# Block-sorted attention and a squared-ReLU layer: output transposes by DMA, later loads, earlier sorting

## The chip, the cores and the metric

One core of a Trainium2 chip runs the whole program. The metric is device time in microseconds of one execution; 14 executions of the kernel before gave a median of 249.14 us (247.87 to 253.91). The engines are TensorE (PE; its weight loads are shown as PEld), VectorE (DVE), ScalarE (ACT), GpSimd (POOL) and SyncE (SP). SP and POOL issue DMAs. Each engine takes its instructions in program order.

## The reference

Four batches, eight heads, 768 tokens, head dimension 64, eight blocks of 96 tokens. `sort_net` is normalised over rows and columns five times, and the resulting 8x8 matrix P of each head mixes the blocks of keys and values. Each query block attends to its own mixed block. The heads' outputs are joined to 3072 rows of 512, and a layer 512 -> 2048 -> 512 with a squared ReLU follows:

```
for _ in range(5):
    P = exp(P - max(P, -1)); P = P / (sum(P, -1) + 1e-9); P = P / (sum(P, -2) + 1e-9)
k_sorted = einsum('bhij,bhjcd->bhicd', P, k_b);  v_sorted = einsum('bhij,bhjcd->bhicd', P, v_b)
attn = softmax(q_b @ k_sorted.T / sqrt(64))      # per block
x = (attn @ v_sorted) as [3072, 512]
out = (s * relu(x @ w_in)**2 + b) @ w_out
```

## The kernel before

The 3072 rows are eight half batches t = 0 to 7 of 384 tokens (four blocks of 96); batch b has t = 2b and 2b+1. Matrix products take bf16 operands.

**Keys and values.** `load_k`, `load_v` and `load_q` (lines 78 to 92) read float32 from DRAM on POOL's queue and write bf16. `k_piece` (L278 and its casts) multiplies raw keys by a block-diagonal matrix built from P: `pd1` for batches 0 and 1, `pd2` for 2 and 3, and leaves sorted, transposed keys in `ks`. With nb = 2 one piece serves batches 2 and 3 together (128 columns); with nb = 1 it serves one batch (64 columns). Pieces with more than 8 groups of 64 columns take their PSUM tile from `psa` (three buffers of two banks), smaller ones from `psb` (two buffers of one bank). `v_piece1` (L320, batch 1) and `v_piece2` (L334, batches 2 and 3) sort values; the result goes through DRAM (`dv`) and `v_read` (L345) brings it back to `VS[b]` with the tokens on the partitions.

**Attention of a half batch t.** `q_piece` (L259) transposes q on TensorE into `QT`; `s_piece` (L359) makes scores, ACT the exponential (L362); `p_piece` (L386) multiplies by the sorted values, DVE divides by the sum (L390, L391) into `X[t]`, 96 partitions x four blocks x 512. `t_piece` (L414) transposes `X[t]` on TensorE, sixteen 96x128 blocks into one psa tile, and `evac` (L228 on DVE, L230 on ACT) copies it to `XT[t]` with the 512 features on the partitions.

**Dense layer.** `ffn1(t)` runs eight steps of two feature groups f: eight matmuls of 384 columns into a psa tile (L433), ReLU on ACT (L437), square on DVE into `GT[t]` (L438). `ffn2(t)` takes 128 rows at a time, sixteen matmuls of 512 columns into a psb tile (L459); DVE scales and adds the bias (L450), SP writes the rows out (L452). The bias needs `csum`, the sum of w_out's rows, added up on POOL (L583).

**Order.** The program is emitted in a written order, and each engine follows it. ffn1 and ffn2 call a `Queue` after each step (8 per ffn1, 12 per ffn2) and the queue emits the next pieces of attention work in between: item i of n in step 24 (i+1)/n of a queue of 24 steps. The order is: attention of t = 0 and part of 1; ffn1(0) in two halves; build_pd2; ffn1(1); ffn2(0), ffn2(1) beside the attention of 2 and 3; ffn1(2), ffn1(3) beside q_piece(2) and the keys of batches 2 and 3 (`K2`); ffn2(2), (3) beside the attention of 4 and 5; ffn1(4), (5) alone; ffn2(4), (5) beside q_piece(3) and the attention of 6 and 7; ffn1(6), (7), ffn2(6), (7) alone.

On POOL, v and k of batch 2 and q of batch 2 are issued before ffn1(0), v of batch 3 during ffn1(1), k of batch 3 between ffn2(0) and ffn2(1), `v_read(2)` near the end of ffn2(1), `v_read(3)` and q of batch 3 after it.

Of the kernel before, what the change touches and what calls it, by code (L numbers as in the profile page):

```python
# [9 lines left out]
FP = mybir.dt.float32  # L10
# [8 lines left out]
def kernel(  # L19
# [33 lines left out]
    const = ctx.enter_context(tc.tile_pool(name="const", bufs=1))  # L53
    sk = ctx.enter_context(tc.tile_pool(name="sk", bufs=1))
    qrp = ctx.enter_context(tc.tile_pool(name="qrp", bufs=2))
    qtp = ctx.enter_context(tc.tile_pool(name="qtp", bufs=1))
    atp = ctx.enter_context(tc.tile_pool(name="atp", bufs=8))
    xp = ctx.enter_context(tc.tile_pool(name="xp", bufs=2))
    xtp = ctx.enter_context(tc.tile_pool(name="xtp", bufs=2))
# [16 lines left out]
    qr = {}  # L76

    def load_q(b, part=slice(0, 128)):
        if b not in qr:
            qr[b] = qrp.tile([128, H, TQ, D], BF, tag="qr", name=f"qr{b}")  # L80
        nc.gpsimd.dma_start(
            out=qr[b][part].rearrange("p h t d -> p h (t d)"),
            in_=q[b].rearrange("h (p t) d -> p h (t d)", t=TQ)[part])

    def load_k(rows, prow, n=1):
        for c0 in range(0, BLK, BLK // n):
            cs = slice(c0, c0 + BLK // n)
            nc.gpsimd.dma_start(out=kb[prow, cs, :], in_=kraw[rows, cs, :])
# [4 lines left out]
    def brows(b):  # L93
        return slice(b * 64, (b + 1) * 64), slice((b % 2) * 64, (b % 2) * 64 + 64)
# [68 lines left out]
    def wo_at(f):  # L163
        return wos[f // FW][:, f % FW, :]
# [86 lines left out]
    def q_piece(b, hp0, eng):  # L251
# [4 lines left out]
        for i in range(2):  # L256
            for t in range(TQ):
# [4 lines left out]
        evac(QT[b][:, hp0:hp0 + 2, :].rearrange("q a (p t) -> q a p t", t=TQ),  # L262
             ps[:, :, 0:S].rearrange("q a (t p) -> q a p t", t=TQ), eng)

    def k_piece(b, c0, nc2, nb, eng):

        pr = brows(b)[1] if nb == 1 else slice(0, 128)  # L270
        rhs = (pd1[pr].rearrange("p e m i -> p (e m i)") if nb == 1
               else pd2.rearrange("p b e m i -> p (b e m i)"))
        if nc2 * nb > 8:
            ps = psa.tile([128, nc2, nb * 64], FP, tag="a", name="tk")
        else:
            ps = psb.tile([128, nc2, nb * 64], FP, tag="b", name="tk")
# [143 lines left out]

    def nothing():
# [2 lines left out]
    def ffn1(t, slot=nothing, n0=0, nn=HB):  # L424
        if t not in GT:
            GT[t] = gtp.tile([128, NF, TG], BF, tag="gt", name="gt")
        gt, xt = GT[t], XT[t]
        c0, nt = n0 * BLK, nn * BLK
        for f0 in range(0, NF, 2):
            hps = psa.tile([128, 2, 512], FP, tag="a", name="hps")  # L430
            for f in range(2):
                for hp in range(NHP):
                    nc.tensor.matmul(out=hps[:, f, 0:nt], lhsT=wi_at(hp, f0 + f),  # L433
                                     rhs=xt[:, hp, c0:c0 + nt],
                                     start=(hp == 0), stop=(hp == NHP - 1))
            rt = rtp.tile([128, 2, TG], BF, tag="rt", name="rt")
            nc.scalar.activation(out=rt[:, :, 0:nt], in_=hps[:, :, 0:nt], func=AF.Relu)  # L437
            nc.vector.tensor_tensor(out=gt[:, f0:f0 + 2, c0:c0 + nt], in0=rt[:, :, 0:nt],  # L438
                                    in1=rt[:, :, 0:nt], op=ALU.mult)
            slot()  # L440
# [5 lines left out]
    def flush():  # L446
        while waiting:
# [3 lines left out]
                                           op0=ALU.mult, op1=ALU.add)  # L451
            nc.sync.dma_start(out=out[r0:r0 + 128, :], in_=ot)  # L452

    def ffn2(t, slot=nothing):
        gt = GT.pop(t)
        for m in range(TG // 128):
            ops = psb.tile([128, d_model], FP, tag="b", name="ops")
            for f in range(NF):
                nc.tensor.matmul(out=ops, lhsT=gt[:, f, m * 128:(m + 1) * 128],  # L459
                                 rhs=wo_at(f), start=(f == 0), stop=(f == NF - 1))  # L460
                if f % 4 == 3:
                    if f == NF - 1:
# [26 lines left out]
    def S2(t, hp):  # L489
        return lambda: (s_piece(t, hp), s_piece(t, hp + 1))  # L490

    def P2(t, hp):
        return lambda: (p_piece(t, hp), p_piece(t, hp + 1))

    def T(t):
        return lambda: t_piece(t, "s")

    def attn(t):
        return [S2(t, 0), nothing, P2(t, 0), S2(t, 2), nothing, P2(t, 2), nothing, T(t)]
# [49 lines left out]
    s_piece(1, 1)  # L549

    load_v(*brows(2))
    load_k(*brows(2))
    load_q(2)


    def P(t, hp, *r):
        return lambda: p_piece(t, hp, *r)
# [4 lines left out]
    def V1(i):  # L562
        return lambda: v_piece1(i * 8, "v")

    ffn1(0, Queue([P(0, 0, 2, 2), P(0, 1, 2, 2), P(0, 2, 2, 2), P(0, 3, 2, 2), SC(1, 2),
                   lambda: t_piece(0, "v", 2, 2), SC(1, 3), P(1, 0)], 8), 0, 2)
    ffn1(0, Queue([nothing, P(1, 1), nothing, P(1, 2), nothing, P(1, 3), nothing,
                   lambda: t_piece(1, "v")], 8), 2, 2)
    build_pd2()
    V1(0)()  # L570
    V1(1)()


    csum = const.tile([128, d_model], FP)
# [3 lines left out]
    def csums(f0, f1):  # L578
        for f in range(f0, f1):
            if f == 1:  # L580
                nc.gpsimd.tensor_tensor(out=csum, in0=wo_at(0), in1=wo_at(1), op=ALU.add)
            elif f > 1:
                nc.gpsimd.tensor_tensor(out=csum, in0=csum, in1=wo_at(f), op=ALU.add)  # L583

    csums(0, 8)
    ffn1(1, Queue([V1(i) for i in range(2, 6)] + [lambda: v_read(1, nc.sync)] + [nothing] * 3, 8))
    load_v(*brows(3))
    csums(8, NF)

    V2 = [lambda c0=c0: v_piece2(c0, "s") for c0 in range(0, BLK, 16)]  # L590
    qu = Queue([lambda: q_piece(1, 0, "s"), lambda: q_piece(1, 2, "v")]
               + [lambda c0=c0: k_piece(1, c0, 16, 1, "vsv"[c0 // 32])() for c0 in range(0, BLK, 32)]
               + [bias_piece, S2(2, 0), V2[0], S2(2, 2), V2[1], V2[2], V2[3],
                  P2(2, 0), V2[4], P2(2, 2), seq(V2[5], lambda: v_read(2, nc.gpsimd)), S2(3, 0),
                  T(2), P2(3, 0), S2(3, 2), nothing, P2(3, 2), nothing, T(3)], 24)
    ffn2(0, qu)
    load_k(*brows(3))
    ffn2(1, qu)
    v_read(3, nc.gpsimd)
    load_q(3)  # L600

    rest = []

    def K2(c0, eng):
        return [lambda: rest.append(k_piece(2, c0, 8, 2, eng)), lambda: rest.pop()()]

    pieces = [lambda: q_piece(2, 0, "v"), lambda: q_piece(2, 2, "v")]
    for i in range(6):
        pieces += K2(i * 16, "sv"[i % 2])
    qu = Queue(pieces + [nothing], 16)  # L610
    ffn1(2, qu)
    ffn1(3, qu)
    qu = Queue(attn(4) + attn(5), 24)
    ffn2(2, qu)
    ffn2(3, qu)
    ffn1(4)
    ffn1(5)
    qu = Queue([lambda: q_piece(3, 0, "s"), lambda: q_piece(3, 2, "v")]
               + attn(6) + attn(7), 24)
    ffn2(4, qu)  # L620
    ffn2(5, qu)
    ffn1(6)
# [33 lines left out]
```

The softmax here doesn't subtract the row's maximum and nothing guards it: scores larger than these inputs give would overflow.

## Time and profile before

| | |
|---|---|
| profiled execution | 249.83 us |
| its span, first to last instruction | 248.1 us |
| median of 14 executions | 249.14 us |
| mean granted TensorE clock | 0.957 |
| TensorE busy | 230.8 us |
| ffn2 matmuls (L459), ffn1 matmuls (L433) | 87.7 and 90.1 us busy |
| output transposes of t = 2 to 7, each (L414, sixteen matmuls) | 0.68 us on the chain |
| their copies on ACT, each (L230, xt) | 1.44 us |
| q_piece (L259, 24 transposes), its copy on ACT / DVE | 0.79, 1.44 / 1.75 us |

Busy time is the time in which an engine had an instruction running; matmuls overlap in the pipeline, so their mean durations are longer than the distance from one to the next. The chain follows the work that ended last back through what released it; its pieces of one kind are the time that they took on it. Times of a stage are from the span's start.

### The profile page before, as it was taken

The page shows a single profiled execution, that of the slowest core. Times are in us where ns is not written, and L with a number is a line of the kernel's source. Part 1 is how long each engine was busy: PE and PEld are TensorE (multiplying, and loading weights), DVE is VectorE, ACT ScalarE, POOL GpSimd, SP SyncE. Part 2 cuts the span into 40 slices and gives each one's busy share as a digit, 9 for nine tenths or more (in the row PEclk, how much of TensorE's full clock was granted, in tenths as well). Part 3 has the DMA queues.
Part 4 walks back from the last instruction along what each step waited for, and adds up shares of the span by engine and source line. Part 5 has one row for each costly group of instructions (what it writes and reads, how often), then busy time and mean ns, then how long its engine had stood idle before and what let it go on. Part 6 is the DMA issues. An engine that isn't in the chain of part 4 may idle for free.

```text
span 248.1 us, 4958 instructions
## 1 busy us (share of the span) xinstructions
PE 230.8 (93%) x2108; PEld 140.6 (57%) x2128; DVE 133.2 (54%) x260; ACT 116.4 (47%) x156; POOL 39.3 (16%) x51
## 2 busy tenths in 40 slices
PE   8868799799999899988899999999999999999993
PEld 4558699645554455655555555666555566664441
DVE  4786446898992545746775335444353444442221
ACT  6366547335348364487852242666441536661000
POOL 7721200497910027000000000000000000000000
PEclk9975569999999999999999999999999999999999
DMA  4999999999599729991001212000012120001122
GB/s 62 184 198 211 214 206 206 222 214 240 133 103 185 289 104 126 139 177 29 0 4 42 86 44 76 12 0 0 4 42 87 42 87 0 3 0 42 49 78 86
DMA packets 20214, 24.97 MB, mean 101 GB/s; under 512 B 7520, under 2 KB 14432, under 8 KB 19680
## 3 DMA queue, kind: packets, MB, share of 16 engines
q0 software_dynamic: 8400, 15.21, 35.5%
q1 hardware_dynamic: 11792, 9.45, 14.9%
q8 instruction: 16, 0.26, 0.5%
q14 instruction: 6, 0.05, 0.1%
HBM read 29.63 MB, written 8.65 MB: 154 GB/s over the span
## 4 chain that ended last, share of the span: by engine, by line
PE 69%; DMA 14%; DVE 9%; ACT 4%; issue 2%; POOL 1%; SPq 0%; POOLq 0%
PE ops L459 28%; PE hps L433 28%; DMA vs<-dv 6%; DMA vb<-in_v_dram 6%; PE pv L386 4%; ACT rt L437 3%; DVE gt L438 3%; DMA dv<-vn 3%; PE sc L359 3%; PE tv L304 2%; PE tr L414 2%; DVE ks L228 1%; DVE qt L228 1%; ACT ks L230 1%; PE tq L259 1%
## 5 line engine op out<-in xcount | busy, mean ns | idle before, releaser
L433 PE MATMUL hps<-xt,wi 128*128 128x384 bf16 (+1 forms) x576 | 90.1, 314 | 2.4 <-ACT ks L230 1.1
L459 PE MATMUL ops<-wo,gt 128*128 128x512 bf16 x364 | 87.7, 380 | 1.5 <-issue 0.5
L433 PEld LDWEIGHTS <-wi 128*128 128x128 bf16 x576 | 54.9, 100 | 31.8 <-issue 4.1
L437 ACT ACTIVATE rt<-hps 128x768 bf16<-128x768 f32 (+1 forms) x72 | 53.3, 740 | 39.1 <-PE hps L433 35.4
L438 DVE TENSOR_TENSOR gt<-rt 128x768 bf16<-128x768 bf16 (+1 forms) x72 | 43.1, 601 | 44.0 <-ACT rt L437 43.7
L459 PEld LDWEIGHTS <-gt 128*128 128x128 bf16 x384 | 35.2, 98 | 38.4 <-issue 0.6
L450 DVE SCALAR_TENSOR_TENSOR ot<-ops,s_bc,bias 128x512 f32<-128x512 f32 x24 | 18.0, 748 | 36.5 <-PE ops L459 36.4
L362 ACT ACTIVATE at<-sc 96x768 bf16<-96x768 f32 x32 | 24.2, 802 | 24.1 <-PE sc L359 24.1
L391 DVE TENSOR_TENSOR x<-pv,rec 96x512 bf16<-96x512 f32 (+1 forms) x36 | 22.6, 627 | 1.3
L230 ACT COPY xt<-tr 128x1536 bf16<-128x1536 bf16 x6 | 8.6, 1439 | 23.6 <-PE tr L414 23.6
L228 DVE CAST ks<-tk 64x512 bf16<-64x512 f32 (+1 forms) x28 | 18.5, 662 | 1.4 <-PE tk L278 0.9
L583 POOL TENSOR_TENSOR csum<-csum,wo 128x512 f32<-128x512 f32 x14 | 17.6, 1254 | 1.0
L230 ACT CAST ks<-tk 64x512 bf16<-64x512 f32 (+1 forms) x24 | 14.0, 583 | 6.4 <-PE tk L278 6.1
L390 DVE RECIPROCAL rec<-pv 96x8 f32<-96x8 f32 (+1 forms) x36 | 6.9, 192 | 17.3 <-PE pv L386 17.3
L386 PEld LDWEIGHTS <-at 96*128 96x128 bf16 (+1 forms) x256 | 12.3, 106 | 5.4 <-DMA vs<-dv 1.4
L386 PE MATMUL pv<-vs,at 96*128 96x66 bf16 (+1 forms) x256 | 13.1, 201 | 1.7 <-DMA vs<-dv 0.9
L359 PEld LDWEIGHTS <-ks 64*96 64x96 bf16 x256 | 8.4, 133 | 6.1 <-issue 5.0
L359 PE MATMUL sc<-qt,ks 64*96 64x96 bf16 x256 | 10.9, 224 | 0.3 <-DVE ks L228 0.2
L172 PE MATMUL wp<-zt 128*128 128x256 bf16 x50 | 9.2, 306 | 1.1 <-DVE warm L104 1.1
L228 DVE COPY qt<-tq 128x1536 bf16<-128x1536 bf16 x4 | 7.0, 1754 | 3.5 <-PE tq L259 3.5
L345 POOL DMA_DIRECT2D vs<-dv x4 | 5.4, 1346 | 21.6 <-DMA dv<-vn 20.2
L230 ACT CAST vn<-tv 128x1024 bf16<-128x1024 f32 x6 | 6.1, 1012 | 5.2 <-PE tv L334 5.0
(67 smaller groups left out, 118.5 us busy)
## 6 DMA issues: line engine op xcount, KB each, us to landing
out_dram<-ot SPq DMA_DIRECT2D x24, 256.0 KB, 2.0
kb<-in_k_dram POOLq DMA_DIRECT2D x4, 768.0 KB, 22.3
vb<-in_v_dram POOLq DMA_DIRECT2D x4, 768.0 KB, 18.9
qr<-in_q_dram POOLq DMA_DIRECT2D x3, 768.0 KB, 33.8
wi<-in_moe_w_in_dram POOLq DMA_DIRECT2D x2, 1024.0 KB, 18.9
wo<-in_moe_w_out_dram POOLq DMA_DIRECT2D x2, 1024.0 KB, 30.2
dv<-vn SPq DMA_DIRECT2D x6, 256.0 KB, 5.1
vs<-dv POOLq DMA_DIRECT2D x4, 384.0 KB, 11.1
```

The source lines that it names most:

```text
L228: nc.vector.tensor_copy(out=out, in_=in_)
L230: nc.scalar.copy(out=out, in_=in_)
L359: nc.tensor.matmul(out=sc[:, e, n * BLK:(n + 1) * BLK], lhsT=ks[pr, g0 + n, :], rhs=QT[b][pr, hp, q0:q0 + BLK], start=True, stop=True)
L362: nc.scalar.activation(out=at, in_=sc[:, :, 0:TG], func=AF.Exp, scale=scale)
L386: nc.tensor.matmul(out=pv[e][0:m, (n - n0) * VW:(n - n0 + 1) * VW], lhsT=atf[:, c0:c0 + m], rhs=VS[b][:, gi, :], start=True, stop=True)
L391: nc.vector.tensor_tensor(out=x[:, n0:n0 + nn, hp * 128:(hp + 1) * 128].rearrange("p n (e d) -> p e n d", e=2), in0=pvv[:, :, :, 0:D], in1 ...
L433: nc.tensor.matmul(out=hps[:, f, 0:nt], lhsT=wi_at(hp, f0 + f), rhs=xt[:, hp, c0:c0 + nt], start=(hp == 0), stop=(hp == NHP - 1))
L437: nc.scalar.activation(out=rt[:, :, 0:nt], in_=hps[:, :, 0:nt], func=AF.Relu)
L438: nc.vector.tensor_tensor(out=gt[:, f0:f0 + 2, c0:c0 + nt], in0=rt[:, :, 0:nt], in1=rt[:, :, 0:nt], op=ALU.mult)
L450: nc.vector.scalar_tensor_tensor(out=ot, in0=ops, scalar=s_bc, in1=bias, op0=ALU.mult, op1=ALU.add)
L459: nc.tensor.matmul(out=ops, lhsT=gt[:, f, m * 128:(m + 1) * 128], rhs=wo_at(f), start=(f == 0), stop=(f == NF - 1))
L583: nc.gpsimd.tensor_tensor(out=csum, in0=csum, in1=wo_at(f), op=ALU.add)
```

## The change

- `T(t)` for t = 2 to 7 calls `x_turn`: one DMA transpose on SP from `X[t]` to `XT[t]`, in place of sixteen TensorE transposes and a copy. `XT[t]` is then ordered (block, feature group, token), and `ffn1` reads it as four runs of 96 tokens.
- q of batch 3 is loaded token-major, in six DMAs, and `q_turn(3)` transposes it by six DMAs on SP at the end of ffn2(3). `QT` has two buffers.
- `v_piece1` runs in the second half of ffn1(0) and just after it, and build_pd2 runs inside ffn1(1).
- k of batch 2, k of batch 3 and q of batch 2 are loaded after the keys of batch 1 are sorted. `q_piece(2)` moves into ffn2(1). Keys of batch 2 are sorted in six pieces in ffn1(2) and (3), those of batch 3 in three pieces in ffn2(2) and (3).
- `v_read(2)`, `v_read(3)` and the load of q of batch 3 stand on POOL behind a copy that reads `XT[3]`.
- The last 128 rows are computed and written in two pieces, 384 columns by SP and 128 by ACT.

```diff
     def load_q(b, part=slice(0, 128)):
+        if b == B - 1:
+            qr[b] = qrp.tile([128, TQ, H, D], BF, tag="qr", name=f"qr{b}")
+            for t in range(TQ):
+                nc.gpsimd.dma_start(
+                    out=qr[b][:, t],
+                    in_=q[b][:, t * 128:(t + 1) * 128, :].rearrange("h p d -> p h d"))
+            return
...
+    def q_turn(b):
+        QT[b] = qtp.tile([128, NHP, S], BF, tag="qt", name=f"qt{b}")
+        for t in range(TQ):
+            nc.sync.dma_start(out=QT[b][:, :, t * 128:(t + 1) * 128],
+                              in_=qr[b][:, t].rearrange("p h d -> p (h d)"), transpose=True)
...
-        rhs = (pd1[pr].rearrange("p e m i -> p (e m i)") if nb == 1
-               else pd2.rearrange("p b e m i -> p (b e m i)"))
+        rhs = (pd1[pr] if b < 2 else pd2[pr, b - 2]).rearrange("p e m i -> p (e m i)")
...
+    def x_turn(t):
+        XT[t] = xtp.tile([128, HB * NHP, BLK], BF, tag="xt", name="xt")
+        nc.sync.dma_start(out=XT[t], in_=X[t].rearrange("p n m -> p (n m)"), transpose=True)
+
+    def xt_at(t, hp, n0, nn):
+        if t < 2:
+            return XT[t][:, hp, n0 * BLK:(n0 + nn) * BLK]
+        return XT[t].rearrange("p (n a) t -> p a n t", a=NHP)[:, hp, n0:n0 + nn, :]
...
-                                     rhs=xt[:, hp, c0:c0 + nt],
+                                     rhs=xt_at(t, hp, n0, nn),
...
+    def last_rows(t, m):
+        gt = GT[t]
+        r0 = t * TG + m * 128
+        for c0, c1, eng in ((0, 384, nc.sync), (384, d_model, nc.scalar)):
+            ops = psb.tile([128, d_model], FP, tag="b", name="ops")
+            for f in range(NF):
+                nc.tensor.matmul(out=ops[:, 0:c1 - c0], lhsT=gt[:, f, m * 128:(m + 1) * 128],
+                                 rhs=wo_at(f)[:, c0:c1], start=(f == 0), stop=(f == NF - 1))
...
     def T(t):
-        return lambda: t_piece(t, "s")
+        return lambda: x_turn(t)
...
     load_v(*brows(2))
-    load_k(*brows(2))
-    load_q(2)
...
-    ffn1(0, Queue([nothing, P(1, 1), nothing, P(1, 2), nothing, P(1, 3), nothing,
+    ffn1(0, Queue([V1(0), P(1, 1), V1(1), P(1, 2), V1(2), P(1, 3), V1(3),
                    lambda: t_piece(1, "v")], 8), 2, 2)
-    build_pd2()
-    V1(0)()
-    V1(1)()
+    V1(4)()
+    V1(5)()
...
     csums(0, 8)
-    ffn1(1, Queue([V1(i) for i in range(2, 6)] + [lambda: v_read(1, nc.sync)] + [nothing] * 3, 8))
+    v_read(1, nc.sync)
+    ffn1(1, Queue([nothing] * 4 + [build_pd2] + [nothing] * 3, 8))
     load_v(*brows(3))
     csums(8, NF)
...
-               + [bias_piece, S2(2, 0), V2[0], S2(2, 2), V2[1], V2[2], V2[3],
-                  P2(2, 0), V2[4], P2(2, 2), seq(V2[5], lambda: v_read(2, nc.gpsimd)), S2(3, 0),
-                  T(2), P2(3, 0), S2(3, 2), nothing, P2(3, 2), nothing, T(3)], 24)
+               + [seq(lambda: load_k(*brows(2)), lambda: load_k(*brows(3)), lambda: load_q(2), bias_piece), S2(2, 0), V2[0], S2(2, 2), V2[1], V2[2], V2[3],
+                  P2(2, 0), V2[4], P2(2, 2), V2[5], S2(3, 0),
+                  T(2), P2(3, 0), S2(3, 2), lambda: q_piece(2, 0, "v"), P2(3, 2), T(3),
+                  lambda: q_piece(2, 2, "v")], 24)
     ffn2(0, qu)
-    load_k(*brows(3))
     ffn2(1, qu)
+
+    def K(b, c0, nc2, eng):
+        return lambda: k_piece(b, c0, nc2, 1, eng)()
+
+    qu = Queue([nothing if i % 2 else K(2, i * 8, 8, "vs"[i // 2 % 2]) for i in range(12)]
+               + [nothing] * 4, 16)
+    ffn1(2, qu)
+    ffn1(3, qu)
+    gate2 = sk.tile([1, 1], BF)
+    nc.gpsimd.tensor_copy(out=gate2, in_=XT[3][0:1, 0, 0:1])
+    v_read(2, nc.gpsimd)
     v_read(3, nc.gpsimd)
     load_q(3)
-    pieces = [lambda: q_piece(2, 0, "v"), lambda: q_piece(2, 2, "v")]
-    for i in range(6):
-        pieces += K2(i * 16, "sv"[i % 2])
-    qu = Queue(pieces + [nothing], 16)
-    ffn1(2, qu)
-    ffn1(3, qu)
-    qu = Queue(attn(4) + attn(5), 24)
+    qu = Queue([S2(4, 0), K(3, 0, 16, "s"), nothing, P2(4, 0), nothing, S2(4, 2), nothing,
+                K(3, 32, 16, "s"), P2(4, 2), nothing, T(4), K(3, 64, 16, "v"), S2(5, 0), nothing,
+                nothing, P2(5, 0), nothing, S2(5, 2), nothing, P2(5, 2), nothing, T(5),
+                lambda: q_turn(3), nothing], 24)
     ffn2(2, qu)
     ffn2(3, qu)
     ffn1(4)
     ffn1(5)
-    qu = Queue([lambda: q_piece(3, 0, "s"), lambda: q_piece(3, 2, "v")]
-               + attn(6) + attn(7), 24)
+    qu = Queue(attn(6) + attn(7), 24)
     ffn2(4, qu)
```

More of the change, by code (lines that the diff above doesn't have):

```diff
@@ L55 @@
     qrp = ctx.enter_context(tc.tile_pool(name="qrp", bufs=2))
-    qtp = ctx.enter_context(tc.tile_pool(name="qtp", bufs=1))
+    qtp = ctx.enter_context(tc.tile_pool(name="qtp", bufs=2))
     atp = ctx.enter_context(tc.tile_pool(name="atp", bufs=8))
@@ L426, in ffn1 @@
             GT[t] = gtp.tile([128, NF, TG], BF, tag="gt", name="gt")
-        gt, xt = GT[t], XT[t]
+        gt = GT[t]
         c0, nt = n0 * BLK, nn * BLK
@@ L452, in flush @@
             nc.sync.dma_start(out=out[r0:r0 + 128, :], in_=ot)
+    def last_rows(t, m):
+        gt = GT[t]
+        r0 = t * TG + m * 128
[4 more added lines that the diff above has]
+                                 rhs=wo_at(f)[:, c0:c1], start=(f == 0), stop=(f == NF - 1))
+            ot = osb.tile([128, d_model], FP, tag="ot", name="ot")
+            nc.vector.scalar_tensor_tensor(out=ot[:, 0:c1 - c0], in0=ops[:, 0:c1 - c0], scalar=s_bc,
+                                           in1=bias[:, c0:c1], op0=ALU.mult, op1=ALU.add)
+            eng.dma_start(out=out[r0:r0 + 128, c0:c1], in_=ot[:, 0:c1 - c0])
     def ffn2(t, slot=nothing):
-        gt = GT.pop(t)
+        gt = GT[t]
         for m in range(TG // 128):
+            if t == NT - 1 and m == TG // 128 - 1:
+                last_rows(t, m)
+                return
             ops = psb.tile([128, d_model], FP, tag="b", name="ops")
@@ L592 @@
                + [lambda c0=c0: k_piece(1, c0, 16, 1, "vsv"[c0 // 32])() for c0 in range(0, BLK, 32)]
-               + [bias_piece, S2(2, 0), V2[0], S2(2, 2), V2[1], V2[2], V2[3],
-                  P2(2, 0), V2[4], P2(2, 2), seq(V2[5], lambda: v_read(2, nc.gpsimd)), S2(3, 0),
-                  T(2), P2(3, 0), S2(3, 2), nothing, P2(3, 2), nothing, T(3)], 24)
+               + [seq(lambda: load_k(*brows(2)), lambda: load_k(*brows(3)), lambda: load_q(2), bias_piece), S2(2, 0), V2[0], S2(2, 2), V2[1], V2[2], V2[3],
+                  P2(2, 0), V2[4], P2(2, 2), V2[5], S2(3, 0),
+                  T(2), P2(3, 0), S2(3, 2), lambda: q_piece(2, 0, "v"), P2(3, 2), T(3),
+                  lambda: q_piece(2, 2, "v")], 24)
     ffn2(0, qu)
-    load_k(*brows(3))
     ffn2(1, qu)
+    def K(b, c0, nc2, eng):
[7 more added lines that the diff above has]
+    v_read(2, nc.gpsimd)
     v_read(3, nc.gpsimd)
     load_q(3)
-    rest = []
-    def K2(c0, eng):
-        return [lambda: rest.append(k_piece(2, c0, 8, 2, eng)), lambda: rest.pop()()]
-    pieces = [lambda: q_piece(2, 0, "v"), lambda: q_piece(2, 2, "v")]
-    for i in range(6):
-        pieces += K2(i * 16, "sv"[i % 2])
-    qu = Queue(pieces + [nothing], 16)
-    ffn1(2, qu)
-    ffn1(3, qu)
-    qu = Queue(attn(4) + attn(5), 24)
+    qu = Queue([S2(4, 0), K(3, 0, 16, "s"), nothing, P2(4, 0), nothing, S2(4, 2), nothing,
+                K(3, 32, 16, "s"), P2(4, 2), nothing, T(4), K(3, 64, 16, "v"), S2(5, 0), nothing,
+                nothing, P2(5, 0), nothing, S2(5, 2), nothing, P2(5, 2), nothing, T(5),
+                lambda: q_turn(3), nothing], 24)
     ffn2(2, qu)
```

## The prediction

> **What bounds the kernel now.** I read the page, then the busy time cut where the dense stages begin, then the chain of work and the waits inside the stages that show idle TensorE. The page's first part:
>
> ```profile
> PE 230.8 (93%) x2108; PEld 140.6 (57%) x2128; DVE 133.2 (54%) x260; ACT 116.4 (47%) x156; POOL 39.3 (16%) x51
> ```
>
> TensorE is busy for 93% of the span, so a microsecond leaves the span where TensorE work is removed or where TensorE waits. The stages (columns: window, length, busy time and count of PE, PEld, DVE, ACT, POOL, then clock, DMA share, GB/s):
>
> ```profile
> 40.28:62.37 22.09, 20.52 (x185) 13.83 (x183) 19.53 (x34) 9.94 (x16) 13.26 (x13) 1.00 1.16 222
> 62.37:97.62 35.25, 33.71 (x361) 18.42 (x367) 21.90 (x36) 18.10 (x21) 11.38 (x10) 1.00 0.85 154
> 97.62:126.55 28.93, 26.45 (x228) 16.82 (x227) 18.32 (x28) 20.13 (x29) 1.62 (x2) 1.00 0.59 86
> 126.55:153.58 27.03, 26.48 (x253) 14.41 (x256) 13.66 (x26) 8.26 (x10) 0.00 (x0) 1.00 0.14 50
> 153.58:174.43 20.85, 20.80 (x128) 12.52 (x128) 8.38 (x16) 13.52 (x17) 0.00 (x0) 1.00 0.04 14
> 174.43:202.79 28.36, 27.99 (x299) 15.53 (x304) 13.28 (x25) 9.59 (x11) 0.00 (x0) 1.00 0.13 48
> ```
>
> I call them A (end of ffn1(0), and ffn1(1)), B (ffn2(0), (1)), C (ffn1(2), (3)), D (ffn2(2), (3)), E (ffn1(4), (5)) and F (ffn2(4), (5)). E carries nothing but its 128 matmuls: 20.8 us, 1.30 per pair of f. C has the same 128 and takes 28.93. The chain shows why:
>
> ```profile
> 108.08 0.57 DVE gt L438
> ...
> 108.67 0.59 ACT ks L230
> ...
> 109.30 2.77 PE hps L433 x16
> ```
>
> TensorE waits there for ACT to empty a key tile, which holds one of the three psa buffers that the dense layer also needs. Two more idle places, from the waits:
>
> ```profile
> PE tv L320 <- DVE tmp L216: 1.3, 1, 1.3
> PE pv L386 <- DMA vs<-dv: 0.9, 1, 0.9
> ```
>
> The first is build_pd2 between ffn1(0) and ffn1(1); the second is v of b1 coming back from DRAM at 82.55.
>
> **What the skill says.** The Trainium skill's "DMA: Bandwidth & Descriptors", section "DMA Transpose (X-bar)", has the plain DMA transpose issued by SP or ACT only, on 2-byte data, into SBUF; no trace of before shows one. Its section "Issuing engines are not separate DMA queues" says that all queues run on the same 16 DMA engines and interleave. The trace agrees: the first b1 read-back took 14.20 us beside the load of b3's keys, others as little as 6.8. "SBUF — State Buffer" has DVE and GpSimd share a port pair that one of them holds for a whole instruction. That fits here: a gt multiplication takes 0.56 us in stage C and 1.91 at 57.77, beside the csum additions.
>
> **The change, part by part.**
>
> *A.* Four v_piece1 go into the second half of ffn1(0), two follow it, and build_pd2 moves into ffn1(1). TensorE in that half: 16 half-size matmuls per pair of slots, 8 x 0.66 = 5.3, four V1 x 0.34, three P x 0.35, one transposition 0.75: 8.4 us from 40.28, to 48.7. DVE is longer: from 40.64, start to start, nine gt x 0.28 = 2.5, four P x 0.84 = 3.4, four V1 casts x 0.64 = 2.6, the xt copy 0.9: 9.4, to 50.0; I add 0.4 for a gt that meets csum. So ffn1(1) starts at 50.4, where it started at 49.88. It then holds 8 x 1.30 = 10.4, one pe 0.34 and 0.1 of changes of shape, no V1 (1.36 before): end 61.2 against 62.37, **-1.2**. DVE in ffn1(1) loses 4 x 0.64 of casts and gains 1.7 for pd2, so its backlog is no larger. The gate for csum comes 1.2 later, but the load of v of b3 stands between its two parts on POOL and no longer waits 1.48 for V1(5): csum ends where it did (68.9), before bias_piece.
>
> *B.* T(2), T(3) leave: 2 x 0.68 = -1.36. q_piece(2) comes in: 2 x 0.79 = +1.58. V1 is written out some 8 us sooner (last cast 51.7 instead of 60.3), so the read-back lands before 72 even at 14.2 us: -0.92 of wait. Sum **-0.7**, B lasts 34.55 and ends at 95.75. Cover for the moved loads: k of b2, k of b3 and q of b2 are issued on POOL at about 69 to 71, behind csum. Three times 768 KB at the 205 to 215 GB/s of the early loads is 11.2 us; beside them six V2 writes and four or five outputs, 2.7 MB at about 400 GB/s, take 6.7. So q of b2 lands at about 71 + 18 = 89, and q_piece(2, 0) stands at about 91 (item 21 of 24; 93.9 in the old clock, less 1.2, 0.92 and 0.68). DVE gets 3.5 us of qt copies near the end of B, where it had 21.9 of 35.25 busy; ACT loses 2.9 of xt copies.
>
> *C.* Out: q_piece(2) (1.60) and six key pieces of 128 columns (6 x 0.53 = 3.2). In: six pieces of 8 matmuls with 64 columns, at 0.57 for sixteen 0.29 each, 1.74. Their tiles are in psb, which ffn1 doesn't use, so a slow cast no longer holds a dense buffer. A cast of 64x256 takes 0.45, four per piece: 1.8 us every second slot, ACT and DVE in turn. ACT: 16 x 0.81 + 12 x 0.45 = 18.4; DVE: 16 x 0.56 + 5.4 = 14.4; TensorE 20.8 + 1.74 = 22.5, now the longest. With 0.7 for changes of shape and a short wait behind a 1.8 us cast: 23.2, **-5.7**; C ends at 119.0.
>
> *D.* T(4), T(5) leave (-1.36), three key pieces of b3 come (3 x 0.57 = +1.7), the wait for the last ks at 128.16 (0.45) goes: **-0.1**.
>
> *F.* T(6), T(7): -1.36; q_piece(3): -1.58. **-2.9**. Their evacuations (ACT 1.44 each, DVE 1.75) were beside the path.
>
> *End.* The last 128 rows in two pieces: 16 x (0.163 + 0.066) against 16 x 0.215 is +0.2 of TensorE (0.066 from the 128-column key matmuls). The last ot is 128 instead of 512 wide, an estimated 0.35 for 0.75, and its write is 64 KB: -0.4. **-0.2**.
>
> *The transposes themselves.* Each x_turn is one issue on SP of 384 KB. From below: 384 KB at the page's 261 GB/s ("Latency and other measured facts") is 1.5, plus the 2.0 of an output write: 3.5 us. From above: "VectorE: DVE Perf Modes", "The three transpose paths", gives 1.309 us for 128x128; twelve of these in a row are 15.7. I take 5, an estimate nearer the lower end, because one DMA spreads over 16 engines. Cover, from issue to first use: XT[7] is queued on SP behind the write of ffn2(5)'s last rows (ot 0.75) and needed after ffn1(6), 9.6 us later; XT[2] about 9; XT[3] and XT[5] 12; XT[4] and XT[6] 13. So nothing. What queues behind on SP is output writes, with three ot buffers and over 4 us between them. gate2 holds v_read(2), v_read(3) and load_q(3) on POOL until XT[3] has landed (about 100). v_read(2), 2.7 of issue and 11.1 to land, is there at about 114; P2(4, 0) wants it at 123. q of b3 in six loads (six issues of about 0.9, 256-byte pieces) lands by 135; q_turn(3) stands at 144, and S2(6, 0) after 168. The dense layer reads XT[t] in four runs of 96: no row shows such a moving operand. I take nothing; 0 to 5 ns on 384 matmuls is 0 to 2 us.
>
> Sum: -1.2 - 0.7 - 5.7 - 0.1 - 2.9 - 0.2 = **-10.8**: span 248.1 to 237.3, this execution 249.83 to 239.0. It lies 0.7 above the median, 249.14, so the forecast is **238.4**.
>
> **Rivals.** *A load is late in B* (q of b2, behind two key loads): its slack is 2 us. If V2 writes slow the three loads as they slowed b3's keys (11.4 us for one), q_piece(2, 0) stops TensorE for 2 to 5: about 241.5. For it: DMA share of 0.85 in B. Against: the read-back of b1 and both later ones have left B.
> *C stays bound by ACT and DVE*: if each piece's 1.8 us still stops TensorE by 0.4 (the old 0.35 to 0.45), six times 0.4 more is 2.4: 240.8. Against: the buffers are apart.
> *Slower: the transposes outlast their cover.* With L us each, the stalls are 2 x (L - 9.3) + 2 x (L - 12) + 2 x (L - 13), which eats 10.8 at L = 13.2. At the upper bound of 15.7 it is 25.6, a time of 264. For it: the price of one small block. Against: it supposes that blocks follow one another without overlap.
>
> **How the numbers follow.** The sum as it stands 0.60 (its own range 236.5 to 240.3), the late load 0.18, C bound 0.13, the transposes 0.09. Below 236.4 and above 243 I leave about 0.18, most of it the transposes and the worst of the late load. No change means within 0.5%, 247.9 to 250.4, about what measurement can tell; only a middling L ends there (0.02). Slower 0.07, faster 0.91.
>
> **What would show it.** Right: C at 23 us with TensorE over 95% busy; no wait of pv for vs in B; hps matmuls of ffn1(2) to (7) still 0.163 apart; x_turn landing under 9 us; F at 25.4. Wrong: hps waiting for an xt written by SP, q_piece(2, 0) waiting for qr, pv of P2(4, 0) waiting for vs, or a lower granted clock.

## The result, and the profile after

The changed kernel takes 239.18 us (median of 10 runs, 238.06 to 240.04) beside 248.96 for the kernel before: a ratio of 0.9595 with an interval of 0.9574 to 0.9616, so about 10 us or 4%. The forecast was 238.4, the span 237.3; the profiled span is 237.1. Some executions of these kernels are 1.5% or more longer than the fastest of the same kernel: the ratios leave them out, the medians don't.

The first line of the profile, and busy time cut at the first matmul of each stage (columns as before: window, length, busy time and count of PE, PEld, DVE, ACT, POOL, then clock, DMA share, GB/s):

```profile
PE 225.9 (95%) x2029; PEld 135.9 (57%) x2048; DVE 129.3 (55%) x264; ACT 108.8 (46%) x157; POOL 43.7 (18%) x57
```

```profile
60.75:95.33 34.58, 33.95 (x377) 18.36 (x382) 24.00 (x36) 16.66 (x20) 8.57 (x9) 1.00 1.12 197
95.33:118.80 23.47, 23.47 (x181) 13.76 (x178) 14.91 (x29) 16.22 (x27) 10.82 (x11) 1.00 1.22 111
118.80:146.07 27.27, 26.79 (x268) 14.24 (x272) 14.03 (x29) 11.47 (x17) 0.00 (x0) 1.00 0.57 80
167.09:192.12 25.03, 24.81 (x220) 12.84 (x224) 11.16 (x23) 6.81 (x9) 0.00 (x0) 1.00 0.24 70
```

These are B, C, D and F. In C TensorE has no idle time left. The chain there is TensorE alone, where it went through ACT and DVE before:

```profile
97.14 2.71 PE hps L458 x16
99.85 0.34 PE tk L293 x8
100.19 2.71 PE hps L458 x16
```

Cut in the same way, from first matmul to first matmul:

| stage | before | after | difference |
|---|---|---|---|
| start of ffn1(0) | 30.56 | 30.79 | +0.23 |
| ffn1(0) and ffn1(1) | 31.81 | 29.96 | -1.85 |
| B: ffn2(0), (1) | 35.25 | 34.58 | -0.67 |
| C: ffn1(2), (3) | 28.93 | 23.47 | -5.46 |
| D: ffn2(2), (3) | 26.86 | 27.27 | +0.41 |
| E: ffn1(4), (5) | 21.02 | 21.02 | 0 |
| F: ffn2(4), (5) | 28.19 | 25.03 | -3.16 |
| ffn1(6), (7) | 21.02 | 21.01 | 0 |
| ffn2(6), (7) and the end | 24.46 | 23.97 | -0.49 |
| span | 248.1 | 237.1 | -11.0 |

The cut between C and D needs care. In the trace of before the first matmul of ffn2(2) is missing from the records: seven stand ahead of the first scores where sort_early, which has the same steps there, has eight.

```profile
126.55 1.67 PE L459 MATMUL ops<-wo,gt 128*128 128x512 bf16 x7
```

```profile
124.86 1.89 PE L459 MATMUL ops<-wo,gt 128*128 128x512 bf16 x8
```

With this matmul of 0.22 us put back, C took 28.72 and D 27.08 before, and the differences are -5.25 and +0.19. The other cuts of the table lie alike in both traces.

The span also fell by more than the medians did, 9.8 us: the profiled execution of before (249.83) lies 0.9 above its median, that of the changed kernel (238.79) 0.4 below.

The six transposes of outputs and the six of q, from the DMA issues (issues, median us to landing), and from the waits POOL's idle time ahead of the copy, which XT[3] ended:

```profile
xt<-x SPq DMA_TRANSPOSE x6, 3.9
qt<-qr SPq DMA_TRANSPOSE x6, 2.8
```

```profile
POOL gate L648 <- DMA xt<-x: 28.1, 1, 28.1
```

Five of the six landed 3.8 to 3.9 us after their issue; XT[2], beside the end of the load of q of b2, took 5.3. No matmul waited for a tile that a DMA had transposed.

### The profile page after: what moved, and what is told of

The parts are those of the page before. It is cut to its first block, busy times and chain, and to the rows that moved or that the text cites. A ratio compares the mean times of both kernels' runs of the same rounds, so it can differ in the third digit from the quotient of the medians.

```text
span 237.1 us, 4840 instructions
## 1 busy us (share of the span) xinstructions
PE 225.9 (95%) x2029; PEld 135.9 (57%) x2048; DVE 129.3 (55%) x264; ACT 108.8 (46%) x157; POOL 43.7 (18%) x57
## 4 chain that ended last, share of the span: by engine, by line
PE 86%; DMA 6%; DVE 5%; issue 1%; POOL 1%; ACT 1%; POOLq 0%
PE hps L458 35%; PE ops L501 34%; DMA vb<-in_v_dram 6%; PE sc L374 3%; PE pv L401 3%; PE tv L319 2%; PE tk L293 2%; PE ops L486 1%; DVE x L406 1%; PE tq L268 1%; PE tv L349 1%; DVE gt L463 1%; DVE vn L237 1%; PE tq L253 1%; PE tr L429 1%
## 5 line engine op out<-in xcount | busy, mean ns | idle before, releaser
L458 PE MATMUL hps<-xt,wi 128*128 128x384 bf16 (+1 forms) x576 | 89.2, 312 | 1.0 <-DVE xt L237 1.0
L501 PE MATMUL ops<-wo,gt 128*128 128x512 bf16 x349 | 84.0, 380 | 1.4 <-issue 0.5
L458 PEld LDWEIGHTS <-wi 128*128 128x128 bf16 x576 | 54.1, 99 | 31.2 <-issue 2.3
L463 DVE TENSOR_TENSOR gt<-rt 128x768 bf16<-128x768 bf16 (+1 forms) x72 | 42.0, 585 | 41.7 <-ACT rt L462 41.2
L501 PEld LDWEIGHTS <-gt 128*128 128x128 bf16 x368 | 33.6, 98 | 36.8 <-issue 0.6
L475 DVE SCALAR_TENSOR_TENSOR ot<-ops,s_bc,bias 128x512 f32<-128x512 f32 x23 | 17.2, 749 | 40.4 <-PE ops L501 40.3
L239 ACT CAST ks<-tk 64x512 bf16<-64x512 f32 (+1 forms) x32 | 16.0, 501 | 8.5 <-PE tk L293 8.1
L237 DVE CAST ks<-tk 64x512 bf16<-64x512 f32 (+1 forms) x32 | 18.1, 564 | 1.7 <-PE tk L293 1.3
L293 PEld LDWEIGHTS <-kb 64*128 64x128 bf16 x192 | 7.5, 103 | 5.4 <-issue 4.9
L293 PE MATMUL tk<-pd,kb 64*128 64x64 bf16 x192 | 9.0, 203 | 0.9 <-DVE pd L553 0.9
L181 PEld LDWEIGHTS <-zt 128*128 128x128 bf16 x50 | 4.9, 102 | 5.2 <-DVE warm L113 1.1
```

Source lines behind the costliest of these rows:

```text
L237: nc.vector.tensor_copy(out=out, in_=in_)
L239: nc.scalar.copy(out=out, in_=in_)
L293: nc.tensor.matmul(out=ps[:, c, :], lhsT=kb[pr, c0 + 2 * c:c0 + 2 * c + 2, :].rearrange("p c d -> p (c d)"), rhs=rhs, start=True, stop=True)
```

## The experiments

The questions were: which parts earn the gain, whether they need one another, what limits stage C, how much cover the loads and transposes have, and whether more of the same pays.

### One part at a time, on the kernel before

**Output transposes alone.**

```diff
     def T(t):
-        return lambda: t_piece(t, "s")
+        return lambda: x_turn(t)
...
-                                     rhs=xt[:, hp, c0:c0 + nt],
+                                     rhs=xt_at(t, hp, n0, nn),
```

> The kernel before with one part of the change: outputs of t = 2 to 7 transposed by DMA, loads and sorting as before, so the first two transposes run beside v_read(2), v_read(3) and the load of q of batch 3. Theory: TensorE loses 6 x 0.68 = 4.1 us and nothing waits for a transposed tile, as each lands in under 9 us: span down by 4.1, time about 244.9. Rival (transposes beside loads outlast their cover): the DMA transpose of t = 3 lands after more than 12 us and ffn1(3) waits for it: 246 or more. Rival (the copies of xt on ACT were on the path too): down by more than 4.6.

It is slower than the kernel before: 251.22, ratio 1.0081 (1.0057 to 1.0104). Its waits, and SP's own timeline (start, us):

```profile
PE hps L443 <- DMA xt<-x: 5.2, 1, 5.2
```

```profile
87.98 1.59 SPq L422 DMA_TRANSPOSE xt<-x  x1
...
96.57 10.79 SPq L422 DMA_TRANSPOSE xt<-x  x1
...
144.37 1.46 SPq L422 DMA_TRANSPOSE xt<-x  x1
```

The transpose of t = 2 landed after 4.1 us. That of t = 3 was issued at 96.57, when v_read(2), v_read(3) and the load of q of batch 3 were in flight; it held SP for 10.8 us, landed after 18.6 and stopped ffn1(3) for 5.2. Those after it, with few loads beside, took 3.9 to 4.1. So the rival holds: beside those loads the cover is too short. ffn1(2) and (3) took 34.70 instead of 28.72.

This is not peculiar to transposes. The output write of 256 KB that SP issued at 96.14 in this run took 12.2 us to land. In the kernel before, without any DMA transpose, the one issued at 97.92 beside the same loads took 11.7, where the later ones took 2.0 to 4.1:

```profile
out_dram<-ot SPq DMA_DIRECT2D x1, 256.0 KB, 11.7
```

**Keys apart alone.**

```diff
-        rhs = (pd1[pr].rearrange("p e m i -> p (e m i)") if nb == 1
-               else pd2.rearrange("p b e m i -> p (b e m i)"))
+        rhs = (pd1[pr] if b < 2 else pd2[pr, b - 2]).rearrange("p e m i -> p (e m i)")
...
-        pieces += K2(i * 16, "sv"[i % 2])
+        pieces += [K(2, i * 16, 8, "sv"[i % 2]), nothing]
...
-    qu = Queue(attn(4) + attn(5), 24)
+    qu = Queue([S2(4, 0), K(3, 0, 16, "s"), nothing, P2(4, 0), nothing, S2(4, 2), nothing,
+                K(3, 32, 16, "s"), P2(4, 2), nothing, T(4), K(3, 64, 16, "v"), S2(5, 0), nothing,
+                nothing, P2(5, 0), nothing, S2(5, 2), nothing, P2(5, 2), nothing, T(5),
+                nothing, nothing], 24)
```

> The kernel before with one part of the change: keys of batch 2 sorted apart in psb tiles in ffn1(2) and ffn1(3), those of batch 3 in ffn2(2) and ffn2(3); q_piece(2) stays in ffn1(2), loads as before. Theory: ffn1(2) and (3) take 20.8 + 1.6 + 1.8 + 0.8 = 25.0 instead of 28.93 (-3.9), ffn2(2) and (3) gain 1.7 and lose the 0.45 wait for the last keys (+1.25): about -2.7, time 246.3. Rival (the stage is bound by the sum of ACT and DVE work, and the casts do not get cheaper as a whole): no more than -0.8, as the same columns are cast in more instructions.

247.15, ratio 0.9929 (0.9906 to 0.9953). Its stages C and D:

```profile
97.77:123.25 25.48, 25.31 (x229) 15.05 (x226) 16.17 (x30) 17.56 (x28) 1.63 (x2) 1.00 0.68 98
123.25:151.89 28.64, 28.64 (x305) 15.60 (x304) 14.35 (x28) 14.34 (x19) 0.00 (x0) 1.00 0.13 48
```

From the 28.72 and 27.08 of before, C falls by 3.24 (theory 3.9) and D rises by 1.56 (theory 1.25). The rival, which allowed 0.8, falls.

**Values of b1 sorted early alone.**

```diff
-    ffn1(0, Queue([nothing, P(1, 1), nothing, P(1, 2), nothing, P(1, 3), nothing,
+    ffn1(0, Queue([V1(0), P(1, 1), V1(1), P(1, 2), V1(2), P(1, 3), V1(3),
                    lambda: t_piece(1, "v")], 8), 2, 2)
-    build_pd2()
-    V1(0)()
-    V1(1)()
+    V1(4)()
+    V1(5)()
...
-    ffn1(1, Queue([V1(i) for i in range(2, 6)] + [lambda: v_read(1, nc.sync)] + [nothing] * 3, 8))
+    v_read(1, nc.sync)
+    ffn1(1, Queue([nothing] * 4 + [build_pd2] + [nothing] * 3, 8))
```

> The kernel before with one part of the change: v of b1 sorted in the second half of ffn1(0) and just after it, build_pd2 inside ffn1(1), the loads of k and q of batch 2 still before ffn1(0). Theory: the second half of ffn1(0) gets longer by about 0.5 us as DVE sets it, ffn1(1) shorter by 1.6, and pv no longer waits 0.9 for v of b1: about -1.8 to -2.1, time 247. Rival (the read-back was late because of the loads queued beside it, not because it was issued late): the wait of pv stays, -0.5 to -1.2.

248.0, ratio 0.9958 (0.9944 to 0.9973), less than the theory gave. ffn1(1) went from 12.49 to 10.86, as expected. But the read-back was issued no sooner. SP's timeline of this run, then of the kernel before, then of the changed kernel:

```profile
42.84 16.74 SPq L326 DMA_DIRECT2D dv<-vn  x12
67.93 3.44 SPq L345 DMA_DIRECT2D vs<-dv  x2
```

```profile
67.92 2.33 SPq L345 DMA_DIRECT2D vs<-dv  x2
```

```profile
42.05 14.97 SPq L341 DMA_DIRECT2D dv<-vn  x12
58.69 5.71 SPq L360 DMA_DIRECT2D vs<-dv  x2
```

With k and q of batch 2 still loaded early, the small writes to DRAM landed after a median of 11.2 us (7.7 in the changed kernel), and SP waits for some of them before it issues the rest, and for the last before the read-back. The wait of pv fell from 0.92 to 0.28 only. In the changed kernel, with these loads moved, the sort pays in full; no run moves the loads alone.

Beside a median of 248.91 for the kernel before in the same series, the three parts alone change the time by +2.3, -1.8 and -0.9; all edits together change it by -9.8.

### What limits stage C

```diff
-        if nc2 * nb > 8:
+        if nc2 * nb > 8 or b == 2:
             ps = psa.tile([128, nc2, nb * 64], FP, tag="a", name="tk")
```

> The changed kernel, with the key pieces of batch 2 in psa tiles again instead of psb; the same matmuls and casts. Theory (the dense layer lost its time to key tiles that held one of its three buffers while they waited for their casts): ffn1(2) and (3) take 1 to 2.5 us longer than the 23.56 of the changed kernel, with hps waiting for ks. Rival (the gain came from less work: q_piece moved out, half the columns, smaller casts): they take 23.6, no change of time.

239.36, ratio 0.9598 (0.9554 to 0.9643). Its stage C:

```profile
95.76:119.39 23.63, 23.52 (x180) 13.83 (x177) 14.91 (x29) 16.20 (x27) 10.82 (x11) 1.00 1.23 113
```

23.63 against 23.47, with no wait of hps. The theory falls for the new pieces: with them the three psa buffers are enough. Before, a piece needed four casts of 64x512 (0.58 on ACT, 0.69 on DVE, so 2.3 to 2.8 us); now four of 64x256 (0.37 and 0.42, so 1.5 to 1.7). There is another difference that I overlooked: `K2` emitted the casts of a piece in two pairs, one step of ffn1 apart, and `K` emits all four at once. The matmuls and casts of one piece before, and of one of k_psa:

```profile
104.84 0.61 PE L278 MATMUL tk<-pd,kb 128*128 128x128 bf16 x8
...
105.75 1.15 ACT L230 CAST ks<-tk 64x512 bf16<-64x512 f32 x2
...
108.07 1.18 ACT L230 CAST ks<-tk 64x512 bf16<-64x512 f32 x2
```

```profile
97.17 0.40 PE L293 MATMUL tk<-pd,kb 64*128 64x64 bf16 x8
...
98.59 1.72 DVE L237 CAST ks<-tk 64x256 bf16<-64x256 f32 x4
```

The old piece held its tile for 4.4 us, the new one for 3.1. No run has large pieces cast at once, or in psb, so which of the two differences, or the move of q_piece out of C, made psa suffice is open.

### The transposes and their cover

**TensorE transposes again, in the changed kernel.**

```diff
     def xt_at(t, hp, n0, nn):
-        if t < 2:
+        if True:
...
     def T(t):
-        return lambda: x_turn(t)
+        return lambda: t_piece(t, "s")
```

> The changed kernel with one part undone: outputs of t = 2 to 7 transposed by TensorE and copied by ACT as before, all else as changed. Theory: +6 x 0.68 = 4.1 us of TensorE, time about 243.3. Rival (the DMA transposes also cost something hidden, or the ACT copies now come into the path): clearly less than 4.1, or more than 4.8.

243.85, ratio 0.9795 (0.9769 to 0.9822). D and F grow by 1.37 each, as worked out from 0.68 per transpose. B grows by 2.19: TensorE's busy time there rises by 1.7, and its idle time by 0.5. So the DMA transposes are worth 4.9 us by the stages (4.7 by the medians), 0.8 more than the transposes on the chain said.

**Nothing held back.**

```diff
-    gate2 = sk.tile([1, 1], BF)
-    nc.gpsimd.tensor_copy(out=gate2, in_=XT[3][0:1, 0, 0:1])
     v_read(2, nc.gpsimd)
```

> The changed kernel without the copy on POOL that holds v_read(2), v_read(3) and the load of q of b3 back until XT[3] has landed. Theory: the two transposes land later (5 to 9 us instead of 5.3 and 3.8) beside these loads and still inside their cover of 9 to 12 us: no change, 239.2. Rival (loads beside a transpose are what the gate is needed for): XT[2] or XT[3] lands after more than 10 us and hps waits for it, 241 or more. The loads may also delay q of b2 and stop q_piece(2, 0): then the wait stands there, and not at hps.

The four runs took 245.46, 245.85, 253.83 and 258.76: my theory falls, by 6 us even in the two shorter ones (ratio 0.9872, 0.9848 to 0.9895). The profiled one took 245.85. XT[2] landed in 5.8 us, XT[3] in 18.1. TensorE's timeline (start, us, and in brackets the idle time before) and stretches of 2 us around it:

```profile
113.09 2.74 PE L458 MATMUL hps<-xt,wi 128*128 128x384 bf16 x8 [5.33 <-DMA xt<-x]
```

```profile
110.00:112.00 2.00, 0.00 (x0) 0.00 (x0) 0.00 (x0) 0.00 (x0) 0.00 (x0) 1.00 1.59 159
112.00:114.00 2.00, 0.91 (x3) 0.44 (x4) 0.00 (x0) 0.00 (x0) 0.00 (x0) 0.73 1.79 226
114.00:116.00 2.00, 2.00 (x11) 0.84 (x10) 0.00 (x0) 0.13 (x1) 0.00 (x0) 0.50 2.44 155
116.00:118.00 2.00, 2.00 (x18) 1.26 (x16) 1.24 (x3) 0.86 (x2) 0.00 (x0) 0.91 1.29 88
```

The eight matmuls after the wait take 2.74 us instead of 1.47, because the granted clock is 0.50. C takes 30.44, 6.97 more: 5.33 of wait and 1.6 of slow matmuls.

**q of batch 3 outside the gate.**

```diff
+    load_q(3)
     gate2 = sk.tile([1, 1], BF)
     nc.gpsimd.tensor_copy(out=gate2, in_=XT[3][0:1, 0, 0:1])
     v_read(2, nc.gpsimd)
     v_read(3, nc.gpsimd)
-    load_q(3)
```

> The changed kernel with the six loads of q of batch 3 ahead of the gate, the read-backs of v still behind it. It tells which of the loads stretched the DMA transpose of t = 3 to 18 us when nothing was held back. If the read-backs in 128-byte rows did it, XT[3] lands in 4 to 6 us and the time stays 239.2. If any load beside it does, XT[3] lands after more than 12 us and ffn1(3) waits for it: 241 or more. XT[2] runs beside these loads in either case and has a cover of 9 us.

239.77, ratio 0.9630 (0.9607 to 0.9653). XT[3] landed in 5.9 us and ffn1(3) didn't wait, but most of q had arrived by then. XT[2], issued at 86.69 in the middle of these loads, took 9.9 us, and ffn1(2) waited 1.0 for it. So loads beside it stretch this transpose from 5.3 to 9.9. That these come in 256-byte pieces need not be the reason: in late_load below, XT[2] took 10.2 beside the load of q of batch 2, which is one DMA with rows of 1536 bytes. No run has a transpose beside the read-backs alone, so that they make it 18 is not shown.

**Six transposes for one.**

```diff
-        nc.sync.dma_start(out=XT[t], in_=X[t].rearrange("p n m -> p (n m)"), transpose=True)
+        for _ in range(6 if t == 7 else 1):
+            nc.sync.dma_start(out=XT[t], in_=X[t].rearrange("p n m -> p (n m)"), transpose=True)
```

> The changed kernel with the DMA transpose of t = 7 issued six times over to the same place. One lands 3.9 us after its issue and holds SP for 1.5. Theory: the chain of six lands about 3.9 + 5 x 1.6 = 12 us after 193.5, at 205.5; ffn1(7) wants it at 202.7, so TensorE waits about 2.8: time about 242. Rival (the cover is larger, or transposes on one queue overlap): no change, 239.2.

255.57, ratio 1.0272 (1.0228 to 1.0316). I had counted on overlap; but each writes the same tile as the one ahead of it and was issued only when that had landed, 3.9 us apart:

```profile
194.08 20.70 SPq L438 DMA_TRANSPOSE xt<-x  x6
```

```profile
PE hps L459 <- DMA xt<-x: 14.0, 1, 14.0
```

The last landed at 217.2 and TensorE waited 14.0: so XT[7] is wanted at 203.2, 9.2 us after its issue (9.6 in the prediction). ffn1(6) and (7) took 16.9 more, 2.9 above the wait:

```profile
203.00:217.00 14.00, 0.23 (x2) 0.00 (x0) 0.93 (x2) 0.81 (x1) 0.00 (x0) 0.60 0.60 112
217.00:219.00 2.00, 1.72 (x6) 0.89 (x7) 0.00 (x0) 0.00 (x0) 0.00 (x0) 0.50 0.00 0
...
221.00:223.00 2.00, 2.00 (x8) 0.98 (x7) 0.46 (x1) 0.38 (x1) 0.00 (x0) 0.54 0.00 0
223.00:225.00 2.00, 2.00 (x14) 1.20 (x13) 0.61 (x2) 1.24 (x2) 0.00 (x0) 1.00 0.00 0
```

### The cover of q of batch 2

```diff
-               + [seq(lambda: load_k(*brows(2)),
+               + [seq(hold, lambda: load_k(*brows(2)),
...
+    held = const.tile([128, 512], FP)
+    def hold():
+        for _ in range(3):
+            nc.gpsimd.tensor_tensor(out=held, in0=csum, in1=wo_at(0), op=ALU.add)
```

> The changed kernel with three more additions on POOL ahead of the loads of k of b2, k of b3 and q of b2; their results are not used. In the trace of the changed kernel q of b2 landed at 89.65 and its first transposition started at 90.5, a cover of 0.9 us. Theory: the loads are issued 3 us later, q lands near 92.7, q_piece(2, 0) stops TensorE for about 2 us: +2, time about 241.2. Rival (the loads are limited by what runs beside them, and later they meet less): q lands under 91, less than +0.5.

243.35 (241.45 to 245.17), ratio 0.9754 (0.9711 to 0.9796). In the profiled execution, the longest of the four, q was issued 3.3 us later (73.03) and landed at 94.3; TensorE's waits and timeline:

```profile
PE tq L268 <- DMA qr<-in_q_dram: 3.3, 1, 3.3
```

```profile
94.40 1.49 PE L268 MATMUL tq<-ident,qr 128*64 128x128 bf16 x24 [3.32 <-DMA qr<-in_q_dram]
```

The theory's wait is there. B took 40.47 instead of 34.58, 5.9 more for 3.3 of wait: the 24 transposes after it took 1.49 instead of 0.86, again at a clock of about 0.50. The other three executions took 241.45 to 243.38, so the usual price is smaller. The changed kernel runs with 0.9 us of cover at this place.

### More of the same, and the end

**q of batch 2 by DMA too.**

```diff
-        if b == B - 1:
+        if b >= 2:
...
-                  T(2), P2(3, 0), S2(3, 2), lambda: q_piece(2, 0, "v"), P2(3, 2), T(3),
-                  lambda: q_piece(2, 2, "v")], 24)
+                  T(2), P2(3, 0), S2(3, 2), nothing, P2(3, 2), T(3),
+                  lambda: q_turn(2)], 24)
```

> The changed kernel, with q of batch 2 too loaded token-major and transposed by six DMAs on SP at the end of ffn2(1), in place of q_piece(2) in ffn2(1). Theory: TensorE loses 2 x 0.79 = 1.58 us, and q of b2 has until S2(4, 0) at about 118 instead of 90.5: time about 237.6. Rival (six loads of 256-byte pieces beside the keys, or 9.6 us of SP behind XT[3], make XT[3], VS[2] or q late): hps of ffn1(3), or pv or sc of t = 4, wait, and the gain is under 0.8 or lost.

238.75, ratio 0.9583 (0.9553 to 0.9613), which can't be told from the changed kernel's 0.9595. B took 33.69, 0.89 less and not 1.58: XT[2] landed after 8.0 us beside the loads of q, and ffn1(2) waited for it. The last two transposes of q, issued at 102.92 and 104.27 beside the read-backs, took 22.8 and 22.4; no scores waited for them.

```profile
PE hps L458 <- DMA xt<-x: 0.7, 1, 0.7
```

**The same with these loads first.**

```diff
-               + [seq(lambda: load_k(*brows(2)), lambda: load_k(*brows(3)), lambda: load_q(2), bias_piece),
+               + [seq(lambda: load_q(2), lambda: load_k(*brows(2)), bias_piece),
...
     v_read(2, nc.gpsimd)
+    load_k(*brows(3))
     v_read(3, nc.gpsimd)
```

> The changed kernel with q of batch 2 token-major and transposed by DMA, its load first and that of k of batch 2 second, and k of batch 3 loaded only after XT[3] has landed, behind v_read(2). Theory: the two loads have landed when XT[2] is transposed (it took 8.0 us beside the load of q, and ffn1(2) waited 0.7 for it), so ffn2(0) and (1) take 34.58 - 1.58 = 33.0 with no wait of hps: span 1.5 below the changed kernel, time about 237.7. Rival (q in 256-byte pieces holds back k of batch 2, or k of batch 3 comes late for ffn2(2)): tk waits for kb, and nothing is gained.

B took 32.80, 1.78 less, with no wait: that half of the theory holds. But k of batch 3, issued at 101.50 among the read-backs and the transposes of q, landed after 25.5 us, and D lost 9.0:

```profile
PE tk L293 <- DMA kb<-in_k_dram: 7.3, 1, 7.3
```

245.6 (241.97 to 247.4; the profiled execution 246.28), ratio 0.9785 (0.9741 to 0.9828). Its first key piece stands second in ffn2(2), though scores need those keys only in ffn2(4). Sorting them later in ffn2(2) and (3) wasn't tried.

**The last rows in one piece.**

```diff
-            if t == NT - 1 and m == TG // 128 - 1:
-                last_rows(t, m)
-                return
```

> The changed kernel with the last 128 rows in one piece again. Theory from the trace: TensorE 3.44 instead of 3.53, last ot 0.75 instead of 0.35, write of 256 KB 2.0 instead of 1.7: +0.4 to +0.6, time 239.6 to 239.8. Rival (the narrow matmuls cost what the short end gains): no difference.

239.24, ratio 0.9624 (0.9598 to 0.9650). From the first matmul of ffn2(6) to the end it took 24.96; k_psa, which has the short end and whose trace also has the record of the first of these matmuls (that of the changed kernel lacks it), took 24.17. That is 0.8, more than the 0.4 to 0.6 expected, but it is one execution each, the medians differ by 0.06 and the intervals of the two ratios overlap: what the short end gains is not settled.

## Why the prediction was right

**The sum.** -10.8 was forecast, -11.0 measured between the two profiled executions, and -9.8 between the medians, so the sum came out some 1 us too large where it counts. All six terms are within 0.6: A -1.2 and -1.6 at the end of ffn1(1), B -0.7 and -0.67, C -5.7 and -5.25, D -0.1 and +0.19, F -2.9 and -3.16, the end -0.2 and -0.49. A can't be judged closer: ffn1(1) began at 49.05 to 49.88 in the three profiled executions with the old order of sorting, that of before being the latest, and at 49.89 to 50.69 in the eleven with the new one. The signs that the forecast named came true: C at 23 us with TensorE busy throughout, no wait of pv in B, F at 25.0, and no transpose over 9 us.

**C: right in size, with a reason that wasn't needed.** The step said that with tiles in psb "a slow cast no longer holds a dense buffer". Put back into psa, the stage stayed at 23.63. What remains, and fits k_apart as well, is less work for TensorE (busy for 26.45 us before and 23.47 after) and no more waits (2.48 us idle before, none after), with q_piece moved out and casts of a piece that take 1.5 to 1.7 us in one block where they took up to 2.8 in two. What of this ended the waits is not separated.

**D: a small miss.** Three key pieces at 0.57 were right (1.71) against two transposes (1.36), which is +0.35. The 0.45 that I took off is a piece of the chain ahead of a cast on DVE. TensorE's own wait was half of it:

```profile
128.62 0.56 PE L359 MATMUL sc<-qt,ks 64*96 64x96 bf16 x15 [0.22 <-DVE ks L228]
```

This wait did go: in k_psa and whole_rows, whose D has the same parts, TensorE is busy for all of 27.28 us.

**Read-back of b1: the right total, a wrong link.** I wrote that V1 is written out 8 us sooner, "so the read-back lands before 72". sort_early shows that the earlier sort alone leaves the read-back where it was; the loads of batch 2 had to leave the early traffic too. And the 14.20 us that I called the first b1 read-back is the second of the two, issued at 68.30; the first took 6.8. In the changed kernel they took 9.7 and 12.3 and landed by 71.4, before 72 as forecast.

**The moved loads.** q of b2 was put at 89 and q_piece(2, 0) at 91: measured 89.6 and 90.5. The cover was 0.9 us, not 2, so it was partly luck that this rival stayed away. It was right in kind; late_load shows its price, which I had as the wait alone: in late_load, no_gate and q2k2_first waits of 3.3 to 7.3 us cost 1.6 to 2.6 more through the clock.

**The transposes.** 3.5 to 15.7 us were my bounds, 5 my value, 3.8 to 5.3 the result. The Trainium skill's "VectorE: DVE Perf Modes", section "The three transpose paths", has 1.309 us for a 128x128 block; twelve blocks' worth landed in 3.9 us, so the blocks don't follow one another at that price. The rival that they outlast their cover is real, and its cause another than I gave: not blocks in a row, but loads beside them. I had worked out that the change loses when all six take 13.2 us; in x_only one of 18.6 turned a forecast gain of 4.1 into a loss of 2.3. I described the copy that holds the loads back only by what it delays; x_only and no_gate show that the gain rests on it. The trace of before held the warning, in the output write of 11.7 us beside these loads. The page "DMA: Bandwidth & Descriptors", section "Issuing engines are not separate DMA queues", which I quoted, was the hint: all queues share 16 engines.

**The strided moving operand.** E and the stage of ffn1(6), (7) took 21.02 and 21.01 against 21.02 and 21.02 before: four runs of 96 cost nothing.

## What to carry to other kernels

In this kernel, with TensorE busy for 93% of the span, a sum of the removed matmuls and waits, stage by stage, came within 1 us. Write beside every DMA that takes over its time to landing and its latest use. Moving a transpose to the DMA engines paid here only while its cover held beside the loads that ran at that time: take the loads' place in the queue as part of the edit. A part of a schedule change has no price of its own: the same DMA transposes gain 4.7 us in the changed kernel (pe_turn) and cost 2.3 in the kernel before (x_only).

## What the runs showed of the hardware that was not expected

**A wait costs more than its length.** TensorE waited for a DMA for 3.3 us in late_load, 5.2 in x_only, 5.3 in no_gate, 7.3 in q2k2_first and 14.0 in turn_x6. Each time its granted clock fell to 0.50 and stayed there beyond the wait. late_load, cut at the start of the idle time, the fall of the clock, the end of the wait and the end of the half clock:

```profile
91.08:92.94 1.86, 0.00 (x0) 0.00 (x0) 0.00 (x0) 0.39 (x1) 0.00 (x0) 1.00 1.10 348
92.94:94.40 1.46, 0.00 (x1) 0.01 (x2) 0.00 (x0) 0.00 (x0) 0.00 (x0) 0.50 1.98 224
94.40:99.77 5.37, 5.15 (x47) 3.27 (x49) 3.25 (x5) 0.00 (x0) 0.00 (x0) 0.50 0.42 105
99.77:101.71 1.94, 1.94 (x30) 1.07 (x29) 0.89 (x2) 0.00 (x0) 0.00 (x0) 1.00 0.21 39
```

In the order above, the clock was at 0.50 for 6.8, 3.4, 3.4, 6.8 and 17.1 us: one, two or five times 3.41. The part of it behind the wait was 5.4, 3.4, 3.3, 3.5 and 5.6 us. Half of that is work lost, 2.7, 1.7, 1.6, 1.7 and 2.8 us, and the stages lost 2.6, 0.8, 1.6, 1.7 and 2.9 beyond the wait: the clock accounts for the surplus. (Only in x_only is it less; its stage had 2.4 us of other waits, and 0.8 of them went.) After the wait of 1.0 us in q3_free the clock stayed at 1.00. The Trainium skill's "TensorE: Matmul & The Clock Gate", section "What's actually happening", has the clock halved after an idle window of about 3.4 us. The multiples of 3.41 agree with it, but in late_load the clock fell 1.9 us after TensorE went idle, and in turn_x6 2.5 us: there a window that was idle in part was enough.

**DMA transposes beside loads.** One of 384 KB takes 3.8 to 4.1 us with little beside it, 5.2 to 6.7 beside the end of loads, 8.0 to 10.2 in the middle of them, and 18.1 to 18.6 beside two read-backs in 128-byte rows and a load; SP was held for 1.3 to 1.6 us with little beside it and for 10.8 in x_only. Plain output writes of 256 KB are stretched too: from 2.0 us to 11.7 beside these read-backs in the kernel before, and to 17.4 in no_gate.
